# Sliding-window attention and a gated FFN on one core: the second token pair's down projections by the seven-product scheme, with the sums of w_out made in the first pair

## The chip, the core and the metric

The kernel runs on one core of a Trainium2 chip. A core has a matrix engine (TensorE, PE in the profile, with its weight loads as PEld), a vector engine (VectorE, DVE), a scalar engine (ScalarE, ACT), a general engine (GpSimd, POOL) and a sync engine (SyncE, SP) that here issues every DMA. Each engine executes its own queue in order. The metric is the device time of one execution in microseconds; a lower time is better. Three runs of the kernel before took 968.94, 970.25 and 970.04 us, a median of 970.04.

## What is computed

Attention over 8 batches of 8 heads, 576 positions and a head size of 64, where a position sees itself and the 63 before it. Its output, as x with 4608 tokens of 512 features, goes through a gated FFN with 1536 hidden units. Everything is fp32; the weights arrive as 64-bit floats.

```python
scores = scale * np.matmul(q, k.transpose(0, 1, 3, 2))
rel = pos[:, None] - pos[None, :]
scores = np.where((rel >= 0) & (rel < 64), scores, -1e9)
attn = softmax(scores)              # max subtracted, sum + 1e-9
x = (attn @ v).transpose(0, 2, 1, 3).reshape(4608, 512)
gate = 1.0 / (1.0 + np.exp(-(x @ w_gate)))
out = gate * (x @ w_val) @ w_out
```

## The kernel before

**Numbers.** An fp32 product is made of three matmuls on split operands, hi·hi, hi·lo and lo·hi (`three`, the matmul on L612). So each operand is split: ACT casts the high part, DVE subtracts it for the low part (`split`, `x_split`, `h_split`).

**Weights.** w_gate, w_val and w_out come in twelve blocks of 128 rows each. `conv_load`, `conv_a`, `conv_b`, `conv_c` (L102-154) load a block as 64-bit values, turn it into fp32 on ACT and DVE, split it, and store the fp32 form to DRAM (`w32d`) for the sums later. w_out's twelve blocks stay on chip as `wo_all` while tiles 0 and 1 run.

**Tokens.** They go in twelve tiles of 384. A tile's attention is done in units (t, p), tile t and one of four pairs of heads p: scores on PE (`scores`, array s), exponentials (`exponentials`: DVE adds the mask and finds the extreme, L243, ACT takes the exponential, L251), division by the sum (`normalize`: L258, L259, L268), transposes on PE (`stage_b`: L300, out pp) with copies on ACT to pT (L305), and the product with v on PE (`outputs`: L329, out oo), copied to xf (L317). PE keeps its instructions in program order (`pe`).

**First pair.** Tiles 0 and 1 go alone and plainly. `up` (L360, out ph) makes 24 products of a block of hidden units, three rotating PSUM banks serve it; ACT makes the gate (`gate_table`, L369, out g), DVE multiplies and splits (`up_val`, L388; `hidden_split`). `down` (L416, out y) accumulates over the twelve blocks. Tile 0's downs go along with the ups; tile 1's follow at the end, and the hidden activations of its blocks 0 to 9 wait in DRAM for that: `put_hidden` stores the two halves into hd, `get_hidden` loads them as hb. A finished y is copied to yo on ACT (L419) and stored (L420). Units (3,1) and (3,3) of the next pair's attention, and the work that prepares pair 1, are interleaved here.

**Pairs 1 to 5** (two tiles each; `s` in the code). The ups use a scheme of Strassen's kind: a 2x2 block product in seven products (`PRODUCTS`, L429) on sums and differences of blocks. The left operands are blocks and sums S1 to S4 of the weights; the right ones are blocks and sums T1 to T4 of x, made by `x_prep` (DVE: t1 and xf, L566, L567, L574), `x_part` and `x_rest` (splits x_T and x_B, L602, L607). `sums_make` (POOL, out sw), `sums_split` (ACT and DVE or POOL, out ws) and `sums_store` make the weights' sums S from DRAM; they are kept in `wd`. `product` (L639) multiplies and `combine` adds up.

**Downs of the pairs.** Pairs 2 to 5 use the same seven products: the sums of w_out are in DRAM (`wod`), `wo_load` fetches them as wot, `h_prep`, `h_early` and `h_part` make the hidden activations' sums and splits, `last_product` (L751) has 7 x 6 x 2 x 3 = 252 matmuls of 384 columns. Pair 1 does it plainly: `plain_part` splits the activations as h_p, `plain_down` has 24 x 2 x 2 x 3 = 288 such matmuls with `wo_all`, of which blocks 10 and 11 were kept in DRAM (`keep_wo`, `fetch_wo`, array kept and wk). During and after these plain downs `wo_sums_load` and `wo_sums` (L481-490) make the sums of w_out in six blocks k = 0 to 5: two loads of 256 KB (wa), seven DVE and three ACT instructions, eight stores of 128 KB.

**What sets the order.** Every step is entered with a time number (`put`, L781); the list is sorted by these numbers, and the instructions of each engine come out in about that order, with small moves by the scheduler. A tile of a pool (`tag`, `bufs`) is taken again only when the last user of its slot is done. Two tags matter: `w32` (three slots) holds fp32 weights, the yo of tiles 0 and 1, and t1; `raw` (six slots) holds 64-bit weights, hb, sw and the sums of w_out.

## Time and profile before

| what | us |
|---|---|
| median of three runs | 970.04 |
| the profiled execution's own time | 968.12 |
| span of its instructions | 966.3 |
| granted TensorE clock | 1.0 of full speed |
| first pair, until its last down | 0 to 212.5 |
| pair 1's ups | 212.5 to 322.5 |
| pair 1's downs | 322.53 to 372.65 |

The page lists the busy time of each engine with its share of the span and its number of instructions. Groups of instructions (line, engine, operation, output <- inputs, form, count | busy us, mean ns | idle time of the engine just before them and what ended it) tell what a step costs. In a timeline each row is a start, a length, the instruction, and in brackets the idle time before it and what it waited for. Idle time of an engine that does not limit the kernel costs nothing by itself. Of the 19.5 us in which PE is idle, 11.31 lie in the first 40 us (7.54 and 3.77 in its halves), 0.70 between 40 and 80, and 3.55 in the last 47.3 us.

### The profile page before, as it was taken

Reading aid. Unit: us, or ns where it says so; the run is one execution under the profiler, and the core shown is the slowest. Engines: PE = TensorE matmul, PEld = TensorE weight load, DVE = VectorE, ACT = ScalarE, POOL = GpSimd, SP = SyncE. Lnnn points to the kernel's source line nnn. Section 1 sums busy time; section 2 is a strip of 40 time slices with the busy share of each in tenths; the row PEclk is TensorE's granted clock in tenths of the full one; section 3 lists DMA queues with packets and bytes.
Section 4 is the critical chain, followed back from the end, with each engine's and each line's share of the span. In section 5 each row is a group of like instructions: output and inputs, shape, how many; then the busy total and the mean of one; then the engine's idle time right before and its main releaser. Section 6 shows DMA issues by size and latency. Waiting matters only on the chain.

```text
span 966.3 us, 20552 instructions
## 1 busy us (share of the span) xinstructions
PE 946.8 (98%) x7200; PEld 904.1 (94%) x7200; DVE 692.8 (72%) x1873; ACT 597.3 (62%) x1479; POOL 141.8 (15%) x232
## 2 busy tenths in 40 slices
PE   6899999999999999999999999999999999999998
PEld 4798999889999999999999999999999999999998
DVE  7889989756776964666876666796566697567782
ACT  7888877647787644666754666664666675222350
POOL 4200103327661000110100111100110100000000
PEclk9999999999999999999999999999999999999999
DMA  9899999948998868889989888878888868988464
GB/s 344 313 384 356 398 353 346 395 165 290 319 305 283 287 205 265 279 259 323 342 265 301 285 257 271 262 258 284 293 264 259 262 212 263 306 252 257 142 211 160
DMA packets 110838, 272.41 MB, mean 282 GB/s; under 512 B 12048, under 2 KB 42896, under 8 KB 110736
## 3 DMA queue, kind: packets, MB, share of 16 engines
q1 hardware_dynamic: 110736, 271.11, 83.2%
q8 instruction: 57, 0.93, 0.4%
q14 instruction: 45, 0.37, 0.1%
HBM read 214.17 MB, written 56.89 MB: 280 GB/s over the span
## 4 chain that ended last, share of the span: by engine, by line
PE 82%; ACT 6%; DVE 5%; DMA 3%; issue 2%; POOL 1%; SPq 0%; DVEq 0%; ACTq 0%
PE pr L612 39%; PE y L612 23%; PE ph L360 6%; PE y L416 4%; PE s L219 3%; PE pp L300 2%; PE s L329 2%; ACT p L251 2%; DMA a<-w32d 1%; DMA w32d<-w 1%; PE oo L329 1%; ACT L251 1%; ACT pT L305 1%; PE pr L329 1%; ACT L369 1%
## 5 line engine op out<-in xcount | busy, mean ns | idle before, releaser
L612 PE MATMUL pr<-x_T,wt 128*128 128x384 f32 x1224 | 227.9, 338 | 0.0
L612 PEld LDWEIGHTS pr<-x_T,wt 128*128 128x128 f32 x1224 | 211.3, 188 | 4.2 <-issue 2.6
L612 PE MATMUL pr<-x_B,wt 128*128 128x384 f32 x1008 | 187.5, 336 | 0.0
L612 PE MATMUL y<-h,wot 128*128 128x384 f32 x1008 | 176.0, 334 | 0.0
L612 PEld LDWEIGHTS pr<-x_B,wt 128*128 128x128 f32 x1008 | 175.0, 188 | 0.6 <-DMA wt<-wd 0.3
L612 PEld LDWEIGHTS y<-h,wot 128*128 128x128 f32 x1008 | 174.6, 188 | 0.5 <-DVE h L655 0.3
L268 POOL TENSOR_TENSOR p<-p,rs 128x384 f32<-128x384 f32 x76 | 66.4, 888 | 567.5 <-DVE rs L259 511.2
L720 ACT CAST h<-h 128x384 fp32r<-128x384 f32 x168 | 82.6, 515 | 67.2 <-PE y L612 34.4
L251 ACT ACTIVATE p<-p,mn 128x128 f32<-128x128 f32 x288 | 111.0, 394 | 6.2 <-DVE mn L243 5.6
L360 PE MATMUL ph<-x,w 128*128 128x384 f32 x576 | 106.2, 338 | 0.1
L721 DVE TENSOR_TENSOR h<-h,h 128x384 fp32r<-128x384 f32 x168 | 88.6, 553 | 24.1 <-ACT h L720 22.7
L360 PEld LDWEIGHTS ph<-x,w 128*128 128x128 f32 x576 | 99.7, 188 | 2.4 <-issue 0.9
L243 DVE CUSTOM_DVE_ANT_0 p<-s,m 128x128 f32<-128x128 f32 x288 | 65.7, 286 | 38.8 <-PE s L219 38.5
L369 ACT ACTIVATE g<-c 128x384 f32<-128x384 f32 x90 | 46.6, 524 | 69.1 <-DVE c L651 68.8
L655 DVE TENSOR_TENSOR h<-c,g 128x384 f32<-128x384 f32 x90 | 55.9, 621 | 29.8 <-ACT g L369 25.5
L369 ACT ACT_TABLE_LOAD x40 | 51.3, 1283 | 13.4 <-DVE c L651 12.8
L305 ACT COPY pT<-pp 128x384 f32<-128x384 f32 x96 | 41.4, 480 | 28.2 <-PE pp L300 28.1
L219 PE MATMUL s<-k,q 64*64 64x128 f32 x1152 | 46.0, 287 | 7.7 <-DMA k<-in_kT_dram 4.9
L622 DVE TENSOR_TENSOR c<-pr,p 128x384 f32<-128x384 f32 x60 | 33.1, 551 | 27.7 <-PE pr L612 27.7
L251 ACT ACT_TABLE_LOAD x39 | 50.0, 1283 | 0.7
L251 ACT ACTIVATION_READ_ACCUMULATOR p<-p,mn 128x1 f32 x264 | 49.9, 189 | 0.0
L219 PEld LDWEIGHTS s<-k,q 64*64 64x64 f32 x1152 | 33.4, 138 | 14.3 <-DMA q<-in_qT_dram 5.2
(113 smaller groups left out, 1326.8 us busy)
## 6 DMA issues: line engine op xcount, KB each, us to landing
wt<-wd SPq DMA_DIRECT2D x186, 512.0 KB, 4.5
wot<-wod SPq DMA_DIRECT2D x84, 512.0 KB, 4.4
v<-in_vN_dram SPq DMA_DIRECT2D x48, 384.0 KB, 5.2
wd<-ws SPq DMA_DIRECT2D x48, 256.0 KB, 4.7
k<-in_kT_dram SPq DMA_DIRECT2D x48, 224.0 KB, 5.2
q<-in_qT_dram SPq DMA_DIRECT2D x48, 192.0 KB, 5.0
w32d<-w SPq DMA_DIRECT2D x36, 256.0 KB, 5.2
wd<-w SPq DMA_DIRECT2D x36, 256.0 KB, 5.6
```

The source lines that it names most:

```text
L219: pe(nc.tensor.matmul(sc[h][half * BLK:(half + 1) * BLK, u, :], qt[h * BLK:(h + 1) * BLK, U * BLK:(U + 1) * BLK], kt[h * BLK:(h + 1) * BLK ...
L243: nc.vector.tensor_tensor_reduce(out=pt[:, u, :], in0=sc[:, u, :], in1=masks[key], op0=ALU.add, op1=ALU.min, scale=-SCALE, scalar=3.0e38, ...
L251: exp = nc.scalar.activation(pt[:, u, :], pt[:, u, :], AF.Exp, bias=mn[:, u:u + 1], scale=-1.0, **sums)
L268: eng.tensor_mul(out=pt, in0=pt, in1=rs.unsqueeze(2).broadcast_to([P, UP, P]))
L305: cp = nc.scalar.copy(pT, pp)
L329: pe(nc.tensor.matmul(oo[U // 2][h * BLK:(h + 1) * BLK, U % 2 * BLK:(U % 2 + 1) * BLK], vt[:, U, h * BLK:(h + 1) * BLK], pT[h][:, U // 2, ...
L360: pe(nc.tensor.matmul(ph, l, r, start=i == 0, stop=i == len(prs) - 1))
L369: act = nc.scalar.activation(g, c, AF.Sigmoid)
L612: pe(nc.tensor.matmul(ps, l, r, start=first and i == 0, stop=last and i == 2, skip_group_check=not check))
L655: nc.vector.tensor_mul(out=hidden(s, k)[2 * r + b], in0=c, in1=gates.pop((t, j)))
L720: nc.scalar.copy(h2[:, 0, :], src)
L721: nc.vector.tensor_sub(out=h2[:, 1, :], in0=src, in1=h2[:, 0, :].bitcast(F32))
```

## The change

Pair 1's downs go by the seven products too, so `plain_part`, `plain_down`, `keep_wo` and `fetch_wo` go. For this the sums of w_out have to be ready earlier: blocks 0 to 3 are put at the end of the first pair, blocks 4 and 5 into pair 1's ups. The plain parts of w_out (`wo_parts`) are stored right after the conversion of their block. The hidden activations of tile 1's blocks 0 to 9 stay on chip: `hidden_split` writes them into slots x10 to x13, e0 to e4 and one of raw, and `put_hidden` and `get_hidden` go. Pair 1 gets the calls of `h_prep`, `h_early`, `h_part` and `wo_load` that the other pairs have.

```diff
+            wo_parts(j)
...
-    hd = dr.tile([NF, P, 2, TT], F32, name="hd")
+    KEEP = 2
...
+        if t == 1 and j < NF - KEEP:
+            pool, tag, bufs = (xp, f"x{10 + j}", 1) if j < 4 else (xp, f"e{j - 4}", 1) if j < 9 else (mp, "raw", RAW)
+            h2 = pool.tile([P, 2, TT], F32R, name=f"h2_{t}_{j}", tag=tag, bufs=bufs)
+            h_hi, h_lo = h2[:, 0, :], h2[:, 1, :]
...
-
-    def put_hidden(t, j):
-        h_hi, h_lo = hh.pop((t, j))
-        nc.sync.dma_start(out=hd[j, :, 0, :], in_=h_hi.bitcast(F32))
-        nc.sync.dma_start(out=hd[j, :, 1, :], in_=h_lo.bitcast(F32))
-
-    def get_hidden(t, j):
-        if j > 5:
-            hb = xp.tile([P, 2, TT], F32R, name=f"hb_{t}_{j}", tag=f"x{10 + (j + 2) % 4}")
-        else:
-            hb = mp.tile([P, 2, TT], F32R, name=f"hb_{t}_{j}", tag="raw", bufs=RAW)
-        nc.sync.dma_start(out=hb.bitcast(F32), in_=hd[j])
-        hh[(t, j)] = (hb[:, 0, :], hb[:, 1, :])
...
-        with tc.issue_after(marks["w_load"]) if s == 2 else nullcontext():
+        with tc.issue_after(marks["w_load"]) if s == 1 else nullcontext():
             nc.sync.dma_start(out=w2.bitcast(F32), in_=wod[q])
...
+    def wo_parts(j):
+        for name, half in (("A12", 0), ("A22", 1)) if j % 2 else (("A11", 0),):
+            nc.sync.dma_start(out=wo_at(j // 2, name),
+                              in_=wo_all[j][:, :, half * H:(half + 1) * H].bitcast(F32))
+
+    def wo_sums_tile(k, n, i):
+        if k < 4:
+            return mp.tile([P, n, DM], F32, name=f"wq{i}_{k}", tag="raw", bufs=RAW)
+        if i is None:
+            return mp.tile([P, n, DM], F32, name=f"wq{i}_{k}", tag="w32", bufs=W32)
+        return wts.tile([P, n, DM], F32, name=f"wq{i}_{k}", tag=f"wo_{i}")
...
-        a = mp.tile([P, 2, DM], F32, name=f"wa_{k}", tag="raw", bufs=RAW)
+        a = wo_sums_tile(k, 2, 5)
         for i in range(2):
-            nc.sync.dma_start(out=a[:, i, :], in_=w32d[2][k + i * NK])
+            with tc.issue_after(marks["conv_load"]):
+                nc.sync.dma_start(out=a[:, i, :], in_=w32d[2][k + i * NK])
...
-        b = mp.tile([P, 4, H], F32, name=f"wb_{k}", tag="raw", bufs=RAW)
-        c = mp.tile([P, 2, H], F32, name=f"wc_{k}", tag="raw", bufs=RAW)
+        b = wo_sums_tile(k, 2, 6).rearrange("p i (a h) -> p (i a) h", a=2)
+        c = wo_sums_tile(k, 1, None).rearrange("p i (a h) -> p (i a) h", a=2)
...
-    def keep_wo(pos):
-        nc.sync.dma_start(out=kept[pos], in_=wo_all[pos].bitcast(F32))
-
-    def fetch_wo(pos):
-        w2 = wts.tile([P, 2, DM], F32R, name=f"wk_{pos}", tag="W", bufs=WB)
-        nc.sync.dma_start(out=w2.bitcast(F32), in_=kept[pos])
-        wo_all[pos] = w2
...
-    def plain_part(i):
-        b, x = divmod(i, NF)
-        k, r = PLAIN[x]
-        hs[i] = h_split(f"p{i}", i, hidden(1, k)[2 * r + b])
...
-    def plain_down(i, part):
-        b, x = divmod(i, NF)
-        k, r = PLAIN[x]
-        for d in ((2, 3) if (part == 1) != (x == NF - 1) else (0, 1)):
-            at, q = (2 * b, 1)[d // 2], d % 2
-            if x == 0:
-                acc[q][at] = psum(1 + q, at, f"y{b}_{d}")
-            ps = acc[q][at][:, :TT]
-            three(ps, wo_all[2 * k + r], d, hs[i], x == 0, x == NF - 1)
-            if x == NF - 1:
-                yo = mp.tile([P, TT], F32, name=f"yo_{b}_{d}", tag="g", bufs=4)
-                nc.scalar.copy(yo, ps)
-                nc.sync.dma_start(out=outT[d * P:(d + 1) * P, b * TT:(b + 1) * TT], in_=yo)
...
-            if t == 1 and j < NF - KEEP:
-                put(now, 9.1, put_hidden, t, j)
...
-        for n, j in enumerate(js):
-            put(now + n * DNT - ready[0], 9.4, ready[1], t, j)
...
-    for x, pos in enumerate(KEPT):
-        put(now - 14 + 4 * x, 8.6, keep_wo, pos)
+    for k in range(NK):
+        put(now - 32 + 10 * k if k < 4 else now + 80 + 8 * (k - 4), 7, wo_sums_load, k)
+        put(now - 24 + 10 * k if k < 4 else now + 88 + 8 * (k - 4), 7, wo_sums, k)
...
-                put(now + 12, 8.6, wo_parts, k)
...
-            if s > 1:
-                put(now + 0.5, 5, h_prep, s, k)
-                if k < EXTRA:
-                    put(now + 3, 5.1, h_early, s, k)
+            put(now + 0.5, 5, h_prep, s, k)
+            if k < EXTRA:
+                put(now + 3, 5.1, h_early, s, k)
...
-        if s == 1:
-            for pos in KEPT:
-                put(t0 - 4, 7, fetch_wo, pos)
-            for i in range(2 * NF):
-                for part in range(2):
-                    at_down.append(now)
-                    put(now, 9, plain_down, i, part)
-                    now += PRT
-                    attend(("d", 2 * i + part))
-            for i in range(2 * NF):
-                put(at_down[2 * i - 38] + 2.3 if i > 18 else t0 - 14.5 if i < EXTRA else t0 - 14.5 + 2.1 * ((i - 5) // 2 + 1) if i < 8
-                    else t0 - 4 if i == 8 else t0 - 0.5, 5.2, plain_part, i)
-            x_parts(at_down[14], lambda x: at_down[max(10 + 2 * x, 18 + x)] + 2.4)
-            for k in range(NK):
-                put(at_down[24] + 4 + 11 * k, 7, wo_sums_load, k)
-                put(at_down[24] + 12 + 11 * k, 7, wo_sums, k)
-            continue
...
-                put(at_down[i - 13] + 1.1 if i > 13 else t0 - 80 + 4 * i if s > 2 else t0 - 48 + 3 * i, 8.2, wo_load, s, i // 2)
+                put(at_down[i - 13] + 1.1 if i > 13 else t0 - 80 + 4 * i if s > 1 else t0 - 18 + 2 * i, 8.2, wo_load, s, i // 2)
```

How it moves instructions, at three places (line numbers behind an L are each kernel's own; a name ends in a running number).

PE at the start of pair 1's downs. In the names y0_0 are a product's sums, h_p0 a plain split of activations, w2_2 a block of w_out on chip. Before:

```order
L612 MATMUL y0_0_4746<-h_p0_4541,w2_2_1172 128x384 x3
L612 MATMUL y0_1_4750<-h_p0_4541,w2_2_1172 128x384 x3
L612 MATMUL y0_2_4754<-h_p0_4541,w2_2_1172 128x384 x3
L612 MATMUL y0_3_4758<-h_p0_4541,w2_2_1172 128x384 x3
L612 MATMUL y0_0_4746<-h_p1_4544,w2_3_1322 128x384 x3
L612 MATMUL y0_1_4750<-h_p1_4544,w2_3_1322 128x384 x3
```

After (h_0_1_0: the first product's activations of pair 1, block 0; wot_1_0: w_out's parts loaded for pair 1):

```order
L599 MATMUL y0_0_1_4839<-h_0_1_0_3469,wot_1_0_4567 128x384 x3
L599 MATMUL y0_1_1_4843<-h_0_1_0_3469,wot_1_0_4567 128x384 x3
L599 MATMUL y0_0_1_4839<-h_0_1_1_3779,wot_1_0_4567 128x384 x3
L599 MATMUL y0_1_1_4843<-h_0_1_1_3779,wot_1_0_4567 128x384 x3
L599 MATMUL y0_0_1_4839<-h_0_1_2_4056,wot_1_1_4649 128x384 x3
L599 MATMUL y0_1_1_4843<-h_0_1_2_4056,wot_1_1_4649 128x384 x3
```

A block of activations has two output tiles instead of four, and the weights come from loads. PE's order is unchanged everywhere else.

ACT between the exponentials of unit (3,1) and its copies to pT. ws0_1_0 and ws2_1_0 are the sums of w_val's block 0, p0_3_1 and p1_3_1 the two halves of the unit's softmax, g the gates. Before:

```order
L251 ACT_TABLE_LOAD
L251 ACTIVATE p0_3_1_2561,rs_3_1_2563<-p0_3_1_2561,mn0_3_1_2562 128x128 x3
L251 ACTIVATE p1_3_1_2573,rs_3_1_2563<-p1_3_1_2573,mn1_3_1_2574 128x128
L157 CAST w2_10_2502<-w32_2_10_2449 128x512
L251 ACTIVATE p1_3_1_2573,rs_3_1_2563<-p1_3_1_2573,mn1_3_1_2574 128x128 x2
L369 ACT_TABLE_LOAD
L369 ACTIVATE g_0_11_2620<-ph0_0_11_2607 128x384
L117 ACTIVATE w32_2_11_2622<-raw_2_11_2545 128x512
L546 CAST ws0_1_0_2929<-sw_1_0_2803 128x2x256
L546 CAST ws2_1_0_2932<-sw_1_0_2803 128x2x256
L157 CAST w2_10_2502<-w32_2_11_2622 128x512
L369 ACTIVATE g_1_11_2688<-ph0_1_11_2675 128x384
```

After (wq6, wq5 and wqNone are the three tiles of a block of w_out's sums, here block 1):

```order
L533 CAST ws2_1_0_2923<-sw_1_0_2783 128x2x256
L370 ACT_TABLE_LOAD
L370 ACTIVATE g_0_11_2603<-ph0_0_11_2590 128x384
L370 ACTIVATE g_1_11_2673<-ph0_1_11_2660 128x384
L589 CAST x_B11_1_0_2881<-xf_2_0_1308 128x384
L589 CAST x_B21_1_0_2939<-xf_2_2_1536 128x384
L589 CAST x_B11_1_1_3008<-xf_2_1_2245 128x384
L589 CAST x_B21_1_1_3069<-xf_2_3_2511 128x384
L482 CAST wq6_1_2945<-wq6_1_2945 128x512
L485 CAST wqNone_1_2946<-wq5_1_2845 128x256
L486 CAST wqNone_1_2946<-wq5_1_2845 128x256
L306 COPY pT0_3_1_2702<-pp0_3_1_2698 128x384
```

The two casts of ws stood behind the exponentials and the gate of block 11; now the first stands ahead of the table load for the exponentials and the second ahead of that for the gate. The three casts of block 1's sums stand ahead of the copies to pT, which nothing of the kind did before.

DVE at the division of unit (3,3), whose quotient PE transposes next. rs is the sum of the exponentials, p0 and p1 the two halves, t1 and xf the differences for pair 1's x, x_T their splits. Before:

```order
L258 SCALAR_TENSOR_TENSOR rs_3_3_2782<-rs_3_3_2782 128x3
L259 RECIPROCAL rs_3_3_2782<-rs_3_3_2782 128x3
L268 TENSOR_TENSOR p0_3_3_2780<-p0_3_3_2780,rs_3_3_2782 128x384
L258 SCALAR_TENSOR_TENSOR rs_3_3_2782<-rs_3_3_2782 128x3
L259 RECIPROCAL rs_3_3_2782<-rs_3_3_2782 128x3
L268 TENSOR_TENSOR p1_3_3_2792<-p1_3_3_2792,rs_3_3_2782 128x384
L566 TENSOR_TENSOR t1_1_0_2868<-xf_3_0_1760,xf_2_0_1316 128x384
L567 TENSOR_TENSOR xf_3_0_1760<-xf_3_2_2029,xf_3_0_1760 128x384
L574 TENSOR_TENSOR xf_2_0_1316<-xf_3_2_2029,t1_1_0_2868 128x384
L607 TENSOR_TENSOR x_T1_1_0_2908<-t1_1_0_2868,x_T1_1_0_2908 128x384
L566 TENSOR_TENSOR t1_1_1_2986<-xf_3_1_2764,xf_2_1_2262 128x384
```

After (p1_3_3's multiplication stands two rows behind the last one shown):

```order
L553 TENSOR_TENSOR t1_1_0_2863<-xf_3_0_1748,xf_2_0_1308 128x384
L269 TENSOR_TENSOR p0_3_3_2760<-p0_3_3_2760,rs_3_3_2762 128x384
L259 SCALAR_TENSOR_TENSOR rs_3_3_2762<-rs_3_3_2762 128x3
L554 TENSOR_TENSOR xf_3_0_1748<-xf_3_2_2017,xf_3_0_1748 128x384
L561 TENSOR_TENSOR xf_2_0_1308<-xf_3_2_2017,t1_1_0_2863 128x384
L553 TENSOR_TENSOR t1_1_1_2999<-xf_3_1_2744,xf_2_1_2245 128x384
L488 TENSOR_TENSOR wq5_2_2983<-wq5_2_2983,wqNone_2_3076 128x256
L489 TENSOR_TENSOR wq5_2_2983<-wq5_2_2983,wqNone_2_3076 128x256
L260 RECIPROCAL rs_3_3_2762<-rs_3_3_2762 128x3
L594 TENSOR_TENSOR x_T1_1_0_2899<-t1_1_0_2863,x_T1_1_0_2899 128x384
L594 TENSOR_TENSOR x_T3_1_0_2930<-xf_3_0_1748,x_T3_1_0_2930 128x384
L594 TENSOR_TENSOR x_T2_1_0_2891<-xf_2_0_1308,x_T2_1_0_2891 128x384
```

t1_1_0 and the work behind it stood after both multiplications; now t1_1_0 stands ahead of p0's and, with the second t1, two rows of block 2's sums and four x_T, ahead of p1's. t1_1_0 takes the slot of the tile yo_0_0 (tag w32), t1_1_1 that of yo_0_1. The store of yo_0_0 stands in SP's queue, before:

```order
L403 DMA hb_1_5_2825<-hd_149 128x768
L455 DMA wd_0_3_153<-ws2_1_0_2932 128x512
L455 DMA wd_0_6_156<-ws2_1_0_2932 128x512
L442 DMA wt_1_0_4_2977<-wd_0_4_154 128x1024
L500 DMA kept_11_214<-w2_10_2502 128x1024
L465 DMA wod_14_206<-w2_10_2502 128x2x256
L465 DMA wod_17_209<-w2_10_2502 128x2x256
L442 DMA wt_1_0_5_3002<-wd_0_5_155 128x1024
L420 DMA out_0_dram<-yo_0_0_2734 128x512
L190 DMA v_4_0_2959<-in_vN_dram 128x768
```

and after:

```order
L470 DMA wq5_2_2983<-w32d_2_2_139 128x512
L470 DMA wq5_2_2983<-w32d_2_8_145 128x512
L434 DMA wt_1_0_5_3014<-wd_0_5_154 128x1024
L492 DMA wod_6_197<-wq6_1_2945 128x256
L492 DMA wod_3_194<-wq6_1_2945 128x256
L492 DMA wod_9_200<-wqNone_1_2946 128x256
L492 DMA wod_18_209<-wqNone_1_2946 128x256
L412 DMA out_0_dram<-yo_0_0_2713 128x512
L412 DMA out_0_dram<-yo_0_1_2722 128x512
```

Ahead of it four stores of block 1's sums and two loads for block 2 have come in, and the loads of hb and the copy to kept have gone.

## Prediction

> **What bounds the kernel now.** I read the busy times first.

> ```profile
> span 966.3 us, 20552 instructions
> PE 946.8 (98%) x7200; PEld 904.1 (94%) x7200; DVE 692.8 (72%) x1873; ACT 597.3 (62%) x1479; POOL 141.8 (15%) x232
> ```

> PE works 946.8 of 966.3 us, so only 19.5 us are idle. Next the windows show where (after the window: its length, then busy time of PE, PEld, DVE, ACT, POOL, granted clock, DMA share, GB/s).

> ```profile
> 160.00:180.00 20.00, 20.00 (x150) 18.39 (x149) 19.25 (x46) 14.36 (x33) 11.12 (x19) 1.00 1.03 378
> 180.00:200.00 20.00, 19.78 (x152) 15.83 (x151) 10.48 (x34) 11.19 (x31) 0.70 (x2) 1.00 0.99 375
> 200.00:213.00 13.00, 13.00 (x79) 10.53 (x78) 8.04 (x24) 5.72 (x20) 4.47 (x7) 1.00 0.17 54
> 300.00:322.50 22.50, 22.50 (x190) 21.53 (x189) 19.35 (x52) 18.52 (x46) 0.00 (x0) 1.00 0.81 282
> 322.50:373.00 50.50, 50.50 (x293) 50.50 (x292) 32.59 (x76) 21.71 (x49) 0.00 (x0) 1.00 0.66 210
> 482.00:526.00 44.00, 44.00 (x254) 44.00 (x255) 33.03 (x67) 22.64 (x47) 0.00 (x0) 1.00 0.86 278
> ```

> From 160 us to the end of pair 1's downs PE is nearly never idle. A matmul taken out there is worth its whole time; a wait put in there costs its whole length. At the end of the first pair (160 to 180) PE is full, DVE has 0.75 us free and the DMA engines are full too. That is where the change puts its new work.

> **What the change takes out.** Third, the chain of waits (start, length, what): pair 1's downs, then pair 2's, which already go by seven products.

> ```profile
> 322.53 50.12 PE y L612 x288
> 481.95 43.88 PE y L612 x252
> ```

> 288 matmuls become 252: 36 × 50.12/288 = 6.27 us by the pair's own price, 50.12 − 43.88 = 6.24 us by pair 2's. I take **−6.24 us**. Pair 2's phase runs with no gap, from parts and weights that are made in the same places of its own ups, and the changed pair 1 has the same order of parts. The recombination (DVE adds, ACT copies) and the further splits lie under PE, as in pair 2's phase, whose window (482 to 526) has PE busy throughout with DVE at 33.03 of 44.00 us. The w_out sums leave pair 1's phase, which is worth nothing, since PE did not wait for them (50.50 of 50.50).

> **What it adds, and where.** Each of the six blocks of w_out sums has these DVE and ACT instructions (six blocks: x6; busy us, mean ns).

> ```profile
> L488 DVE TENSOR_TENSOR wb<-wb 128x512 f32<-128x512 f32 x6 | 4.1, 688 | 0.2
> L481 DVE TENSOR_TENSOR wb<-wa 128x256 f32<-128x256 f32 x6 | 2.5, 424 | 14.4 <-DMA wa<-w32d 14.4
> L483 ACT CAST wb<-wb 128x512 fp32r<-128x512 f32 x6 | 3.7, 622 | 17.3 <-DVE wb L482 14.7 <-issue 2.6
> L487 ACT CAST wc<-wa 128x256 fp32r<-128x256 f32 x6 | 2.4, 403 | 0.2 <-DVE wa L485 0.2
> ```

> One block is six of 0.42 and one of 0.69 us on DVE, 3.2 us, and 0.62 + 2 × 0.40 = 1.4 us on ACT, with ten DMA issues. Blocks 3 to 5 run behind the last softmax step of the first pair or in pair 1's ups, after a stretch (200 to 213) with a DMA share of 0.17 and DVE busy 8.04 of 13 us; I count nothing for them, and should that cover be gone a block costs its 3.2 us. Blocks 0 to 2 stand in the DVE queue among the last softmax steps of the first pair, and PE's next steps hang on those. Two places matter.

> First, unit (3,1): PE's last two steps for it, and ACT's copies between.

> ```profile
> 179.88 0.82 PE L300 MATMUL pp<-ident,p 128*128 128x128 f32 x6
> 182.80 0.92 PE L329 MATMUL oo<-pT,v 128*64 128x64 f32 x24
> 181.62 0.86 ACT L305 COPY pT<-pp 128x384 f32<-128x384 f32 x2
> 182.36 1.09 ACT L419 COPY yo<-y 128x512 f32<-128x512 f32 x2
> 176.35 0.62 ACT L546 CAST ws<-sw 128x512 fp32r<-128x512 f32 x1 [1.17 <-POOL sw L534]
> ```

> In the new ACT order the first cast of ws_1_0, which waited for POOL here (1.17 us), stands ahead of the exponentials of (3,1), and block 1's three casts (1.4 us) ahead of the pT copies. I put the pT copies 1.9 us later, at 183.5: PE loses 1 to 1.5 us at its oo step, and the copy of the first output yo_0_0 ends near 184.8.

> Second, unit (3,3), the larger term. PE wants its normalised p at 193.42; DVE had finished it 4.5 us before, and then waited for a store of yo_0_0, because the tile t1 takes the store's buffer.

> ```profile
> 193.42 0.82 PE L300 MATMUL pp<-ident,p 128*128 128x128 f32 x6
> 188.42 0.56 DVE L268 TENSOR_TENSOR p<-p,rs 128x384 f32<-128x384 f32 x1
> 195.20 0.56 DVE L566 TENSOR_TENSOR t<-xf,xf 128x384 f32<-128x384 f32 x1 [6.23 <-DMA out_dram<-yo]
> 195.80 0.56 DVE L567 TENSOR_TENSOR xf<-xf,xf 128x384 f32<-128x384 f32 x1
> 196.27 0.55 DVE L574 TENSOR_TENSOR xf<-xf,t 128x384 f32<-128x384 f32 x1
> 188.13 0.63 SPq L420 DMA_DIRECT2D out_dram<-yo  x1
> ```

> The store went out at 188.13 and let t1 go at 195.20, 7.07 us later. In the new order of DVE t1 stands **in front of** both multiplications of p_3_3, so a wait that cost nothing is now ahead of PE's need. Between t1's start and the end of p1_3_3's multiplication stand t1, p0's multiplication, two xf, the second t1 and four x_T (nine of 0.53 by the steps from 195.20 to 196.27, 4.8 us), two block-2 sums (0.8), two short ones (0.4) and p1's own 0.56: 6.6 us. PE reaches p1's transposes at 193.42 + 0.41 = 193.83. If t1 starts at T, PE stands for T + 6.6 − 193.83 = **T − 187.2 us**.

> T is when yo_0_0's store is done, and SP's one queue decides that.

> ```profile
> 170.56 1.26 SPq L455 DMA_DIRECT2D wd<-ws  x2
> 168.11 4.04 POOL L553 TENSOR_TENSOR ws<-sw,ws 128x128 fp32r<-128x128 f32 x8 [6.42 <-ACT ws L546]
> ```

> From the first store of ws_0_0 (170.56) to yo_0_0's (188.13) SP issued 21 DMAs, 6.75 MB by their sizes, in 17.57 us. After the change 32 stand there, smaller, 7.0 MB: the hb loads and the copies to "kept" go, 12 stores of sums and four loads for them come. By the bytes the stretch keeps its length, but it starts earlier: POOL idled 6.42 us before it splits ws_0_0, for a cast that now stands earlier on ACT; I give it 4 us of that. Then the store could go at 184.1, and the copy (184.8) bounds it: issue at about 185.5, T = 185.5 + 7.07 = 192.6, and the stall is 5.4 us. The 1 to 1.5 us at (3,1) are inside it, since T does not move with PE.

> The bounds: with the landing of the quickest load below (4.4 us) T is 189.9 and the stall 2.7 us; with the copy as early as now (182.36 + 0.56) and a landing of 5.2 us T is 188.1 and the stall 0.9 us. From above, T as before, 195.20, gives 8.0 us, and rival D more. I take 5.4: its landing is that of the very same store. (Columns below: KB each, median us to landing.)

> ```profile
> wot<-wod SPq DMA_DIRECT2D x84, 512.0 KB, 4.4
> w32d<-w SPq DMA_DIRECT2D x36, 256.0 KB, 5.2
> hb<-hd SPq DMA_DIRECT2D x10, 384.0 KB, 5.7
> L416 PE MATMUL y<-w,hb 128*128 128x512 f32 x90 | 21.3, 393 | 0.0
> ```

> The round trip of the activations through DRAM (hd, loaded as hb) costs PE nothing today: the matmuls that read hb have 0.0 us of idle time ahead of them. Keeping h on chip therefore gains only room in SP's queue, which is counted above.

> One more price: two-input DVE instructions while POOL works.

> ```profile
> 199.30 1.39 POOL L532 TENSOR_TENSOR sw<-a 128x128 f32<-128x128 f32 x2 [21.69 <-DVE t L566]
> 201.76 0.81 DVE L607 TENSOR_TENSOR x_T<-t,x_T 128x384 fp32r<-128x384 f32 x1
> 198.13 0.56 DVE L607 TENSOR_TENSOR x_T<-t,x_T 128x384 fp32r<-128x384 f32 x1 [1.30 <-ACT x_T L602]
> ```

> Beside POOL's sums the same x_T takes 0.81 instead of 0.56 us. If POOL's sw_0_1 falls onto the eight rows ahead of p1, that is 8 × 0.25 = 2.0 us more; its loads now stand behind block 2's stores on SP, later than those rows, so I leave it out of the sum and in the range. [...]

> **The sum.** −6.24 + 5.4 = −0.8 us: 967.3 for an execution like the profiled one (968.12, its span 966.3), which lies 1.92 under the median of 970.04; on the median, **969.2 us**. A measurement of this kernel can tell about 0.2% (1.94 us) from no change, so this is "within".

> **Rivals.**

> A, the forecast: T between 191.5 and 195.4, stall 4.3 to 8.2, time 968.1 to 972.0. For it: t1's place in DVE's order and the 6.23 us wait are both there. Chance 0.45.

> B, the store lands early or p1 is not delayed: stall under 4.3. With T = 189.9 the time is 970.04 − 6.24 + 2.7 = 966.5; with no stall at all 963.8. For it: SP loses 384 and 512 KB transfers, and stores of the old sums landed in 2.0 us once the queue was light. Against: the DMA share is 0.99 from 180 to 200. Chance 0.30.

> ```profile
> wod<-wb SPq DMA_DIRECT2D x24, 128.0 KB, 2.0
> ```

> [...]

> C, the change does not do what it says: pair 1's downs do not reach 43.88 us, because the weights of sums 4 and 5, made late in its ups, come late. DVE is busy 19.35 of 22.5 us there, the fullest stretch of the pair. Each such wait gives back 1 to 3 us on top of A. It is inside the chances of A and D.

> D, slower, one mechanism: the 32 rows in SP's queue go at the old pace for each DMA, 17.57/21 = 0.84 us, not at the old pace for bytes. From 166.6 the store then goes at 193.4, T = 200.5, the stall is 13.3 us and the time 970.04 − 6.24 + 13.3 = 977.1. It decides from T = 195.4 on (stall 8.2 us, the store issued after 188.3); half way, T = 197, gives 973.6. For it: waits for a full queue stretch SP's issues here (1.26 us for two). Against: the new stores have half the size. Chance 0.25.

> **How the numbers follow.** Likeliest is A, at 969.2. B below 965.0 holds about 0.08 and D above 973.5 about 0.12, so the range is 965.0 to 973.5; it takes in stalls from 1.2 to 9.7 us. Faster by over 0.2% (under 968.1) is B, 0.30; within, A, 0.45; slower (over 972.0), D, 0.25.

> **What will show it.** Pair 1's downs: one piece of 252 matmuls of about 43.9 us in the chain; over 45 is C. PE's row of transposes after 36 y matmuls, near 195 to 200: an idle time of 4 to 6 us that ends with the DVE multiplication of p, and DVE's t row just before it with a wait for the output's store. If that t row shows no wait, or PE no gap there, A is wrong and B holds. If the store's issue on SP comes after 188.3, D holds. A gap of more than 2 us at oo of (3,1) would make the first place the larger one.

## The result, and the profile after

The changed kernel takes **982.45 us** (median of four runs, 980.19 to 984.12) beside 969.49 us before on the same chip: ratio 1.0132 with a 95% interval of 1.0109 to 1.0155. It is slower, and lies above the forecast range of 965.0 to 973.5 us. The profiled execution took 982.93 us, its span is 981.1. The head of the page:

```profile
span 981.1 us, 20488 instructions
PE 951.8 (97%) x7164; PEld 906.6 (92%) x7164; DVE 720.7 (73%) x1925; ACT 604.1 (62%) x1493; POOL 146.3 (15%) x232
```

PE's busy time should have fallen by the 6.24 us of the removed matmuls, to 940.6 us. It rose to 951.8, so the 36 matmuls are gone and the others took 11.2 us more; and PE is idle 29.3 us instead of 19.5. The chain of waits (start, length, what) says that the removal itself went as forecast:

```profile
343.13 43.88 PE y L599 x252
```

Pair 1's downs are one piece of 252 matmuls of 43.88 us, but it starts at 343.13 instead of 322.53: 20.6 us were lost ahead of it. The windows show three of the places (window: length, busy time of PE, PEld, DVE, ACT, POOL, granted clock, DMA share, GB/s):

```profile
60.00:80.00 20.00, 16.48 (x122) 14.65 (x121) 17.84 (x43) 15.97 (x37) 2.07 (x2) 0.91 1.03 362
160.00:180.00 20.00, 16.89 (x116) 15.21 (x115) 17.60 (x31) 10.26 (x20) 13.47 (x22) 0.83 0.82 282
300.00:322.50 22.50, 20.77 (x150) 19.77 (x149) 17.50 (x51) 17.16 (x49) 7.93 (x16) 0.92 0.84 283
```

From 160 to 180 us PE was busy 20.00 of 20 us before; now it is 16.89, and the granted clock, 1.00 in every window of before that was shown, is 0.83. What PE waits for, first in before and then in the changed kernel, from 60 to 340 us (us in all, times, longest):

```profile
PE s L219 <- ACT xf L317: 1.6, 3, 1.0
PE s L329 <- ACT pT L305: 0.6, 1, 0.6
PE pr L612 <- DVE ws L548: 0.6, 1, 0.6
```

```profile
PE s L220 <- ACT xf L318: 4.4, 3, 3.4
PE oo L330 <- ACT pT L306: 3.1, 2, 2.7
PE pr L599 <- DVE ws L535: 2.1, 2, 1.7
PE s L330 <- ACT pT L306: 2.0, 2, 1.7
PE pp L301 <- DVE p L269: 1.4, 1, 1.4
```

The place of the forecast, pp waiting for DVE's p, is the smallest of the five. To date the loss, I compare the starts of PE's transposes (pp) of the same unit in both traces:

| stretch | before, us | after, us | lost |
|---|---|---|---|
| 67.4 to 160.4 in before: place A | 93.07 | 98.91 | +5.8 |
| 160.4 to 179.9: place B | 19.44 | 25.69 | +6.25 |
| 179.9 to 216.7: with unit (3,3), the place of the forecast | 36.86 | 38.31 | +1.45 |
| 216.7 to 316.7: pair 1's ups | 99.95 | 106.94 | +7.0 |
| 316.7 to 381.9: with pair 1's downs | 65.17 | 58.95 | −6.2 |

**Place A.** ACT's timeline of the changed kernel, then the row of before that answers to its last one (start, length, instruction, in brackets the idle time before it):

```profile
74.97 0.66 ACT L117 ACTIVATE w<-raw 128x512 f32<-128x512 f32 x1
75.83 0.62 ACT L158 CAST w<-w 128x512 fp32r<-128x512 f32 x1 [0.20 <-DVE w L130]
76.35 0.68 ACT L118 ACTIVATE raw<-raw 128x512 int32<-128x512 uint32 x1
76.92 0.46 ACT L318 COPY xf<-oo 128x384 f32<-128x384 f32 x1
```

```profile
73.41 0.46 ACT L317 COPY xf<-oo 128x384 f32<-128x384 f32 x1
```

Steps of weight conversion, one of which waits for DVE, now stand between the end of PE's input (73.71) and the copy of unit (2,0), for which PE waits: the copy starts 3.2 us after that end, where before it started 0.2 us after it. PE's rows here and at place B:

```profile
77.43 1.55 PE L220 MATMUL s<-k,q 64*64 64x128 f32 x22 [3.36 <-ACT xf L318]
171.92 0.47 PE L330 MATMUL oo<-pT,v 128*64 128x64 f32 x2 [2.69 <-ACT pT L306]
```

**Place B** is the second row. ACT at that place:

```profile
167.30 0.62 ACT L158 CAST w<-w 128x512 fp32r<-128x512 f32 x1 [2.36 <-DVE w L130]
169.75 0.67 ACT L117 ACTIVATE w<-raw 128x512 f32<-128x512 f32 x1 [1.83 <-DMA raw<-in_moe_w_out_dram]
171.39 0.48 ACT L306 COPY pT<-pp 128x384 f32<-128x384 f32 x1
```

(Two more steps, from 170.33 to 171.49, stand between the last two rows.) The conversion of w_out's block 11 waits there for its load, and the copy of pT for unit (2,3), which needs nothing of it, stands behind. In before it ran as soon as PE had made its input, ahead of that conversion:

```profile
160.97 0.86 ACT L305 COPY pT<-pp 128x384 f32<-128x384 f32 x2 [1.24 <-PE pp L300]
```

**The clock.** Each of the four longest waits from 60 to 340 us (3.36, 2.69, 1.66 and 1.73 us) is followed by matmuls at half clock. The rows of single microseconds (length, PE busy, granted clock, DMA share, GB/s):

```profile
75.00:76.00 1.00, 0.00 (x0) 1.00 0.93 340
76.00:77.00 1.00, 0.00 (x0) 0.68 0.93 369
82.00:83.00 1.00, 1.00 (x4) 0.50 1.00 386
83.00:84.00 1.00, 1.00 (x7) 0.91 1.02 379
171.00:172.00 1.00, 0.08 (x1) 0.96 0.91 319
267.00:268.00 1.00, 1.00 (x26) 0.75 0.50 139
308.00:309.00 1.00, 0.86 (x3) 0.73 0.82 281
```

0.68 in a microsecond means half clock from 76.36 on, 0.91 means until 83.18: 6.82 us. In the same way the others begin at 171.92 (6.83 us), 267.50 (3.41) and 308.46 (3.41). Together 20.5 us at half clock, of which PE stood still for 1.5: some 9.5 us lost, most of the 11.2. With the 9.8 us of more idle time and the gain of 6.24 this makes the difference of the spans.

### The profile page after: what moved, and what is told of

Read it like the earlier page. It is cut to its first block, busy times and chain, and to the rows that moved or that the text cites. A ratio compares the mean times of both kernels' runs of the same rounds, so it can differ in the third digit from the quotient of the medians.

```text
span 981.1 us, 20488 instructions
## 1 busy us (share of the span) xinstructions
PE 951.8 (97%) x7164; PEld 906.6 (92%) x7164; DVE 720.7 (73%) x1925; ACT 604.1 (62%) x1493; POOL 146.3 (15%) x232
## 4 chain that ended last, share of the span: by engine, by line
PE 68%; ACT 12%; DVE 10%; DMA 4%; issue 3%; SPq 0%; DVEq 0%; ACTq 0%
PE pr L599 33%; PE y L599 22%; ACT p L252 4%; PE s L220 3%; PE ph L361 3%; PE y L408 2%; ACT L370 2%; PE s L330 2%; PE pp L301 2%; ACT L252 2%; DMA w32d<-w 1%; ACT g L370 1%; DVE w L130 1%; DVE c L638 1%; DVE h L642 1%
## 5 line engine op out<-in xcount | busy, mean ns | idle before, releaser
L599 PE MATMUL y<-h,wot 128*128 128x384 f32 x1260 | 219.9, 334 | 0.0
L599 PEld LDWEIGHTS y<-h,wot 128*128 128x128 f32 x1260 | 218.2, 188 | 0.6 <-DVE h L642 0.3
L681 ACT CAST h<-h 128x384 fp32r<-128x384 f32 x210 | 103.1, 514 | 83.6 <-PE y L599 42.3
L682 DVE TENSOR_TENSOR h<-h,h 128x384 fp32r<-128x384 f32 x210 | 111.0, 555 | 28.8 <-ACT h L681 28.0
L220 PE MATMUL s<-k,q 64*64 64x128 f32 x1152 | 47.7, 294 | 11.5 <-DMA k<-in_kT_dram 6.0
L220 PEld LDWEIGHTS s<-k,q 64*64 64x64 f32 x1152 | 34.8, 142 | 18.5 <-DMA q<-in_qT_dram 5.3
## 6 DMA issues: line engine op xcount, KB each, us to landing
wt<-wd SPq DMA_DIRECT2D x186, 512.0 KB, 4.5
wot<-wod SPq DMA_DIRECT2D x105, 512.0 KB, 4.8
v<-in_vN_dram SPq DMA_DIRECT2D x48, 384.0 KB, 5.1
wd<-ws SPq DMA_DIRECT2D x48, 256.0 KB, 4.7
w32d<-w SPq DMA_DIRECT2D x36, 256.0 KB, 4.8
wd<-w SPq DMA_DIRECT2D x36, 256.0 KB, 6.2
```

The source lines that it names most:

```text
L220: pe(nc.tensor.matmul(sc[h][half * BLK:(half + 1) * BLK, u, :], qt[h * BLK:(h + 1) * BLK, U * BLK:(U + 1) * BLK], kt[h * BLK:(h + 1) * BLK ...
L599: pe(nc.tensor.matmul(ps, l, r, start=first and i == 0, stop=last and i == 2, skip_group_check=not check))
L681: nc.scalar.copy(h2[:, 0, :], src)
L682: nc.vector.tensor_sub(out=h2[:, 1, :], in0=src, in1=h2[:, 0, :].bitcast(F32))
```

## The experiments

All times but that of the six gaps are medians beside runs of before on the same chip, and losses are by the stretches of the table above. Each edit is shown by a few of its lines alone. I held theory **O**: without the stores of the activations ACT's order changes, and A and B follow from that order alone. The rival **S**: the sums of w_out, made early, take the place on DVE, ACT and SP.

**Only the activations kept on chip** (before, without its stores and loads of hd, nothing of the sums):

```
-    put(now, 9.1, put_hidden, t, j)
+    h2 = pool.tile([P, 2, TT], F32R, name=f"h2_{t}_{j}", tag=tag, bufs=bufs)
```

> The kernel before with one part of the change alone: the hidden activations of tile 1's blocks 0 to 9 stay on chip, and their stores and loads go; the sums of w_out and pair 1's plain downs stay as before. Theory O (order: with the twenty stores gone, the scheduler puts the weight conversions of the first pair ahead of the pT and xf copies in ACT's queue, and PE waits there): the two gaps of the change's profile come back, PE 5 to 6 us later from 75 to 91 us and another 6 us from 166 to 192, and with no gain in the downs the time is 969.5 + 11.4 = about 981 us. Rival S (the early sums of w_out load DVE, ACT and SP at the end of the first pair): no sums stand there, so no gap, 968 to 970.5 us.

979.94 us, 1.0097 (1.0071 to 1.0123). A loses 5.4 us, B 4.4, the rest 1.5. The part of the change that I had priced at nothing makes 9.8 of the 12.1 us at A and B by itself, which is about half of what the changed kernel loses ahead of the downs.

**The round trip put back, the sums as changed:**

```
+    put(now + n * DNT - ready[0], 9.4, ready[1], t, j)
```

> The changed kernel with the round trip of the hidden activations through DRAM put back; the early sums and pair 1's seven-product downs stay. Theory O: no gap at 75 to 91 nor at 166 to 192; what stays is the loss of some 1.5 us at unit (3,3) and of some 7 us in pair 1's ups, so 969.5 - 6.2 + 1.5 + 7 = about 972 us, and below 966 if the loss in the ups also goes. Rival S: the gap at 166 to 192 stays, with the loss in the ups 969.5 - 6.2 + 6.2 + 8.5 = about 978 us.

981.14 us, 1.0109 (1.0086 to 1.0132). Both theories missed the total, but A and B are gone (−0.4 and 0.0 us), as O said. Instead (3,3) loses 3.5 and pair 1's ups 15.3 us, with three stretches of half clock in them (3.41 us each, from 235.20, 245.44 and 306.88 us): there is a second cause, in the ups.

**The changed kernel with the 20 stores again, which nobody reads:**

```
+    def put_hidden(t, j):
+        nc.sync.dma_start(out=hd[j, :, 0, :], in_=h_hi.bitcast(F32))
+        nc.sync.dma_start(out=hd[j, :, 1, :], in_=h_lo.bitcast(F32))
```

> The changed kernel, hidden activations on chip as in the change, with the twenty stores to DRAM issued as well though nobody reads them. It does more work than the change. Theory O: the stores alone bring ACT's order of the first pair's middle back, so no gap at 75 to 91, and the time falls by 5 us or more against the change, to 970 to 977 us. Rival B (the buffers that the activations hold on chip are what delays the weight loads): the gaps stay and the time is that of the change, 982 us, or a little above.

972.83 us, 1.0031 (1.0020 to 1.0042): 9.6 us less than the changed kernel, with 20 DMAs more. A loses 0.0, B 1.5 and (3,3) 1.3; the ups still lose 7.1, with a granted clock of 1.00 throughout.

**The sums made in pair 1's ups:**

```
-    put(now - 32 + 10 * k if k < 4 else now + 80 + 8 * (k - 4), 7, wo_sums_load, k)
+    put(now + 20 + 14 * k, 7, wo_sums_load, k)
```

> The changed kernel with all six blocks of sums of w_out in pair 1's ups (one block each 14 us of the order's numbers), none in the first pair. Theory O: the gap at 75 to 91 stays at 5 to 6 us and that at 166 to 192 for the most part, as ACT's order there keeps the conversions ahead of the copies; the ups lose as much as before or more, 978 to 986 us. Rival S: the gap at 166 to 192 and the wait at unit (3,3) go, so 982.5 - 7.7 = about 975 us.

1005.66 us, 1.0365 (1.0340 to 1.0391), a miss. A and B stay, so the sums don't cause them; but the weights come too late for the downs, whose wait says it:

```profile
PE y L597 <- DMA wot<-wod: 18.7, 1, 18.7
```

**A and B by order alone, first try** (the weight conversion held behind ACT's copy, at two places):

```
+    HOLD = {6: ("xf", 2, 2), 11: ("pT", 2, 3)}
+    behind.enter_context(tc.issue_after(marks[("copy",) + HOLD[j]]))
```

> The changed kernel, no stores added, with one constraint on ACT: the conversion of w_gate's and w_val's block 6 may not stand ahead of the copy xf of unit (2,2), and w_out's block 11 not ahead of the pT copies of unit (2,3). If ACT's order alone makes the gaps, the one at 75 to 91 us goes (-5.3) and that at 166 to 192 shrinks or goes (0 to -4, since three other casts still stand ahead there): 973 to 977 us. If it is not the order but the queue of transfers that the missing stores change, it stays at 982 us.

978.79 us, 1.0090 (1.0075 to 1.0105), a miss: B fell from 6.25 to 1.2 us, but I had held the wrong unit at A, which is (2,0) and not (2,2), and A rose from 5.8 to 7.7.

**The same with the right unit:**

```
+    HOLD = {(3, 2, "a"): ("xf", 2, 0), (4, 1, "c"): ("xf", 2, 0),
+            (4, 2, "a"): ("xf", 2, 0), (11, 2, "a"): ("pT", 2, 3)}
```

> The changed kernel with one difference of order: the ACT conversions of w_out's blocks 3 and 4 and the cast of the value weights' block 4 stand behind the copy of xf_2_0, and the activations of w_out's block 11 stand behind the copies of pT of unit (2,3); nothing is added or left out. Theory O (ACT's order costs 5.7 us at 67 to 91 us and 6.25 us at 160 to 192 us): both go but for about 1 us at the second, 982.4 - 5.7 - 5.2 = 971.5 us (970 to 973.5), and the gap at L220 of the first falls from 3.36 us to under 1 us. Rival (the conversions' place is only where another shortage shows, and the gap moves): 975 us or more.

973.37 us, 1.0032 (1.0017 to 1.0047): 9.1 us less than the changed kernel, with the same instructions. A is 1.2, B 0.7 us. ACT and PE at A:

```profile
74.24 0.47 ACT L319 COPY xf<-oo 128x384 f32<-128x384 f32 x1
```

```profile
74.76 0.88 PE L220 MATMUL s<-k,q 64*64 64x128 f32 x22 [1.12 <-ACT xf L319]
```

The copy starts 1.0 us after PE has made its input (73.28) instead of 3.2, the wait falls from 3.36 to 1.12 us (0.35 in before), and the 22 matmuls take 0.88 instead of 1.55. That ACT's order causes A and B is shown. That it hangs on the stores is shown as well; why the scheduler, which goes by its own times, orders ACT so without them, I did not look into.

**The ups, without the sums** (dead stores; every load of w_out's sums reads a part that is there, so that the sums of w_out are left out):

```
-    put(now - 24 + 10 * k if k < 4 else now + 88 + 8 * (k - 4), 7, wo_sums, k)
```

> The kernel of the dead stores without any sums of w_out: their loads, DVE and ACT instructions and stores are left out, and the downs load written parts in their place (the output is not the reference's; the downs of all pairs use wrong weights of the same size). If the sums' own work costs what the dead stores' kernel still loses (2.8 us at the end of the first pair, 7 us in pair 1's ups), those losses go and the time is the forecast gain alone, 969.9 - 6.2 = 963.7, at most 965.5 us. If the preparation of the hidden activations that pair 1's ups now hold costs the 7 us, they stay, and the time is 968 to 971 us.

969.95 us, 1.0002 (0.9993 to 1.0011). The ups still lose 6.8 us: the sums are not what fills them. One row of DVE, and some of POOL's beside it, stand out:

```profile
224.46 4.82 DVE L648 TENSOR_TENSOR h<-c,g 128x384 f32<-128x384 f32 x1
```

```profile
223.82 1.72 POOL L546 TENSOR_TENSOR ws<-sw,ws 128x128 fp32r<-128x128 f32 x4
225.49 0.87 POOL L525 TENSOR_TENSOR sw<-a 128x128 f32<-128x128 f32 x2
227.98 0.89 POOL L531 TENSOR_TENSOR sw<-a,sw 128x128 f32<-128x128 f32 x2
```

This multiplication takes 0.56 us elsewhere. POOL worked without a pause from 218.8 to 228.9, and it ended 0.4 us later. Such a row need not be dear: in the run with the activations alone one took 5.03 us, and its ups lost 1.6.

**Block 5's sums sooner** (dead stores; on DVE block 5 moves from 291 to 305 us to 238 to 262, blocks 4 and 5 still stand in the ups):

```
+    put(now - 32 + 10 * k, 7, wo_sums_load, k)
```

> The kernel of the dead stores with blocks 4 and 5 of the sums 10 us of the order's numbers apart from the others (as blocks 0 to 3 are) instead of late in pair 1's ups. In DVE's queue only block 5 moves, from the fifth to the second of the six steps of the ups. If the sums' place in DVE's and SP's queues makes the loss in the ups, the wait near 298 us (2.3 us, the sums of w_val late) goes and the time falls by 2 to 5 us against the dead stores' 972.8, to 968 to 971; if it is their mere work, the time stays within 1.5 us of 972.8.

974.27 us, 1.0043 (1.0027 to 1.0060): the ups lose 10.3 us, more than the 7.1 with block 5 late. So the late place of block 5 does not make the loss; a kernel with dead stores and all six blocks ahead of the ups was not run.

**Without the sums and without the subtractions of the hidden activations** (both are left out, the products read the plain activations):

```
-        differences(nc.vector, b11, b12, b22, t1)
```

> The kernel with the dead stores and without the sums of w_out, and with pair 1's three subtractions for each k (differences, T2) left out as well: 18 of DVE's two-input operations less while pair 1's ups run; the products read the plain activations in their place. Theory H (these subtractions hold up DVE's serving of the ups): of the 6.8 us lost there in the kernel without sums at least 4 go, 963.5 to 966 us. Rival (the splits into high and low halves, which stay, or the earlier order of ACT hold it up): 968 to 970.5 us, the stretch from 230 to 337 us still over 4 us longer than before's.

969.41 us, 0.9991 (0.9979 to 1.0004): hardly a gain over the run without sums (969.95), so it isn't these instructions alone. The ups lose 5.1 us in this trace, and again one row of DVE lasts until POOL, busy from 238.9, stops at 249.0; this one has six elements for each partition:

```profile
245.90 3.10 DVE L259 SCALAR_TENSOR_TENSOR rs<-rs 128x6 f32<-128x6 f32 x1 [1.65 <-ACT p L252]
```

**Without POOL's sums, in the kernel with the two holds** (POOL's work on the gate and value weights of pair 1 is left out, the casts read the loaded weights):

```
-            nc.gpsimd.tensor_add(out=sw[:, 0, c], in0=a2[:, c], in1=a2[:, d])
+        sw = [a.rearrange("p (a h) -> p a h", a=2) for a in (a1, a2)]
```

> The kernel with the two holds on ACT (973.4 us), with all of POOL's work on the gate and value weights' sums in pair 1 left out: the casts read the loaded weights in place of the sums, and the gate's low halves are read from the high ones. DVE's and ACT's instructions stay. Theory C (in pair 1's ups the added work loses time because POOL's sums hold up DVE's two-input instructions, and because the casts of ws wait for POOL): of the 7.9 us that the stretch from unit (3,3) to the downs is longer than before's at least 5 go, 966 to 968.5 us, and no two-input DVE instruction is over 1 us there. Rival (DVE and ACT have too much to do in the ups by themselves): over 4 us of the 7.9 stay, 970.5 us or more.

976.10 us, 1.0063 (1.0040 to 1.0086), a miss in the total. In the middle of the ups, from the transposes at 216.74 to those at 303.47 in before, it lost 1.2 us where the kernel with the holds lost 5.4. That is what theory C expects of this part, but I chose the part afterwards; by the numbers that I had named the rival came true, for from (3,3) to the downs the kernel lost 12.0 us, where C had under 3. Two other waits came up:

```profile
199.48 0.52 PE L301 MATMUL pp<-ident,p 128*128 128x128 f32 x3 [2.60 <-DVE p L269]
325.86 3.67 PE L592 MATMUL pr<-x_T,ws 128*128 128x384 f32 x12 [3.92 <-DVE u L602]
```

At the first, (3,3), block 2's sums and t1 stand ahead of p on DVE; at the second, block 5's sum, which waits 2.34 us for its load, and the subtractions of h stand ahead of u. With the half clock behind both (3.41 us each, from 200.23 and 326.52) they took back more than was won.

**Without the sums and without POOL's** (the kernel with the dead stores; both left out):

```
-        put(now - 24 + 10 * k if k < 4 else now + 88 + 8 * (k - 4), 7, wo_sums, k)
-            nc.gpsimd.tensor_add(out=sw[:, 0, c], in0=a2[:, c], in1=a2[:, d])
```

> The kernel with the dead stores and without the sums of w_out (969.95 us; between unit (3,3) and the downs it takes 6.8 us more than before), with POOL's work on pair 1's weight sums left out too: the casts read the loaded weights in place of the sums. What pair 1's ups then have that before's don't is the subtractions and splits of the hidden activations on DVE and ACT. Theory C (POOL's sums hold up DVE, and ws waits for them): under 2.5 us of the 6.8 stay, no two-input DVE instruction over 1.5 us there, 964.5 to 966.5 us. Rival (DVE and ACT are too full by themselves): over 4 us stay, 968 us or more.

963.76 us, 0.9943 (0.9926 to 0.9961): 6.2 us less than with POOL's sums, and about the gain of the downs below before. The ups lose 1.6 us, and B, where the run without the sums still lost 1.7, loses nothing. The ups as one window, first in before, then in the changed kernel, then without the sums, then without POOL's as well:

```profile
216.70:316.70 100.00, 98.57 (x837) 93.58 (x836) 70.30 (x206) 75.56 (x195) 52.85 (x112) 1.00 0.89 301
```

```profile
230.30:337.30 107.00, 102.23 (x837) 96.31 (x835) 86.22 (x236) 77.44 (x203) 57.27 (x112) 0.97 0.90 308
```

```profile
218.20:324.90 106.70, 100.98 (x835) 94.94 (x834) 82.78 (x220) 74.84 (x195) 56.55 (x112) 0.98 0.83 280
```

```profile
216.60:318.20 101.60, 99.36 (x837) 93.38 (x836) 73.25 (x220) 74.72 (x195) 0.00 (x0) 1.00 0.87 293
```

The matmuls are the same (835 to 837 records). The same 220 DVE instructions take 82.78 us beside POOL and 73.25 without it, 9.5 us more, and PE's stretch is 5.2 us longer. The casts of ws no longer wait for POOL in that kernel; how much of the 5.2 us is that and how much the slower DVE, no run tells apart. Before has as much of POOL's work in its ups (52.85 us) but not the added work on DVE: POOL's sums and the added work cost little each without the other, and 6.8 us together.

**The clock by itself** (before, with ACT copies in place between two halves of a product, 1, 2, 3, 4, 6 and 9 of them, at six places):

```
+    STALL = {(2, 1, 3): 1, (2, 5, 3): 2, (3, 1, 3): 3, (3, 5, 3): 4, (4, 1, 3): 6, (4, 5, 3): 9}
+    nc.scalar.copy(part, part.bitcast(F32))
```

> The kernel before, with 1, 2, 3, 4, 6 and 9 ACT copies of a 128x128 piece in place between the two halves of one product, at six places of the later pairs' downs some 20 us or more apart, so that PE stands still for some 0.8 to 2.6 us there. Theory G (a gap of about 1.5 us or more is followed by some microseconds at half clock): the places with 4 copies or more show granted clock 0.5 in the microseconds behind the gap and cost 2 to 3 us more than the gap, those with 1 to 3 copies cost their gap alone; the whole is 14 to 18 us longer than before. Rival (the half clock of the earlier runs came from what PE did there, not from the gap): no clock below 1.0 in these stretches, some 8 to 10 us longer.

981.37 us in a single run beside 969.20. The waits were 0.39, 0.77, 1.05, 1.43, 2.04 and 3.08 us, and theory G failed in this form: only the last was followed by half clock. PE's rows of the two longest, and the clock behind the last:

```profile
805.69 25.24 PE L612 MATMUL y<-h,wot 128*128 128x384 f32 x144 [2.04 <-ACT h L762]
834.01 2.49 PE L612 MATMUL y<-h,wot 128*128 128x384 f32 x9 [3.08 <-ACT h L762]
```

```profile
834.00:835.00 1.00, 0.99 (x5) 0.98 0.01 4
835.00:836.00 1.00, 1.00 (x5) 0.50 0.14 37
```

144 matmuls behind the wait of 2.04 us took 25.24 us, 0.175 each, as the 252 of 43.88 us do at a granted clock of 1.00, though waits of 1.66 and 1.73 us in the changed kernel had been followed by half clock. What decides is told in the last section.

## Why the prediction was wrong

**The gain was right.** "I take −6.24 us" for 288 matmuls that become 252: 43.88 us measured, and within 0.4 us of it in every run of these downs that had its weights in time.

**The step that failed most** is "The round trip of the activations through DRAM … costs PE nothing today … Keeping h on chip therefore gains only room in SP's queue". That it gains nothing by itself was right. But I priced what goes as if all else stayed where it was. Without the 20 stores the order of ACT came out another way at two places, where weight conversions moved ahead of copies that PE waits for: 5.8 and 6.25 us. I had read the changed order of DVE and ACT only where the sums of w_out stand; A lies 100 us before them. The run with the activations alone, the one with dead stores and the one with two holds show it from three sides.

**The price of a wait.** "A matmul taken out there is worth its whole time; a wait put in there costs its whole length" was too low for long waits. A's wait of 3.36 us and B's of 2.69 and 0.42 cost 5.8 and 6.25, because 6.8 us at half clock went with each (some 2.9 and 3.2 us, half of the time that PE worked in them).

**The term at (3,3) was mis-sized.** Forecast: 5.4 us. DVE, SP and PE at that place in the changed kernel:

```profile
201.61 0.53 DVE L553 TENSOR_TENSOR t<-xf,xf 128x384 f32<-128x384 f32 x1
202.06 0.55 DVE L269 TENSOR_TENSOR p<-p,rs 128x384 f32<-128x384 f32 x1
206.62 0.55 DVE L269 TENSOR_TENSOR p<-p,rs 128x384 f32<-128x384 f32 x1
```

```profile
195.44 2.40 SPq L412 DMA_DIRECT2D out_dram<-yo  x3
```

```profile
207.31 0.52 PE L301 MATMUL pp<-ident,p 128*128 128x128 f32 x3 [1.36 <-DVE p L269]
```

The order is as forecast, t1 ahead of both multiplications, and 5.6 us lie between the start of the first t1 and the end of p1's multiplication, where I had 6.6. But t1's row shows no wait: the store landed at 200.26, 4.8 us after its issue instead of 7.07. PE came 12.0 us late by A and B; less that, t1 started at 189.6, where I had 192.6. Those 3.0 us and the 1.0 us of shorter work are why 1.36 us of waiting were left of 5.4: by the sign that I had named, rival B held here. At (3,1), where I had 1 to 1.5 us, PE's oo step shows no wait. Across the runs in which A and B are mostly gone the stretch with (3,3) lost −0.1 us without the sums of w_out and 1.3 to 4.8 us with them, the most where p1 waited 2.60 us.

**The ups, which I had counted as nothing**, lost 7.0 us. "Blocks 3 to 5 run … in pair 1's ups … I count nothing" rested on DVE's free time there, and "the changed pair 1 has the same order of parts" on pair 2's ups. There POOL has next to nothing to do, as their window in before shows (13.51 of 108.90 us; 52.85 of 100.00 in pair 1's):

```profile
373.00:481.90 108.90, 108.43 (x935) 103.48 (x934) 74.54 (x228) 73.84 (x201) 13.51 (x16) 1.00 0.91 311
```

In the changed kernel PE waits 4.7 us in the ups instead of 1.2, 2.1 of them for ws and 2.0 for pT, and two steps of half clock take 3.4 more: that is the 7.0. DVE's work there rose from 70.30 to 86.22 us, and by the times of the runs without POOL (0.42, 0.69 and 0.55 us each) the 30 instructions more make some 15 of these 15.9. So the price that I had left out of the sum, DVE's two-input instructions beside POOL (0.81 instead of 0.56 us at one row), adds little to this rise. Shown is that without POOL's sums the loss falls from 6.8 to 1.6 us in the kernel without the sums of w_out. For the kernel with the two holds the run without POOL shows it for the middle of the ups alone (5.4 to 1.2 us); what its last 13 us and (3,3) would cost with another order of DVE was not tried.

One path that the experiments leave open is SP's order. Four more stores of ws and one more load stand ahead of the last load for POOL's sums, which in before goes out ahead of them. First the load in before, then in the changed kernel, and POOL behind it:

```profile
276.87 0.32 SPq L522 DMA_DIRECT2D a<-w32d  x1
```

```profile
298.17 0.38 SPq L509 DMA_DIRECT2D a<-w32d  x1
302.41 0.88 POOL L519 TENSOR_TENSOR sw<-a 128x128 f32<-128x128 f32 x2 [3.81 <-DMA a<-w32d]
```

Counted from the start of each one's stretch, the load goes out 7.7 us later and POOL begins its last block 6.2 us later (at 282.57 in before); PE's wait of 1.73 us for ws, with a step of half clock behind it, follows at 308.14. No run has this order alone put back, so how much of the 7.0 us hangs on it stays open.

**Rivals.** C did not hold for the downs (43.88). D's sign came true, the store's issue at 195.44 being after 188.3, but less the 12.0 us of A and B it is 183.4. SP took 22.5 us for the 32 rows, between the 17.6 of the forecast and D's 26.8, and PE waited 1.36 us where D has 13.3. That the time came out on D's side, slower, is therefore luck. None of the rivals had the order of ACT in it.

No kernel tried beats before while it computes everything; the nearest is the changed one with dead stores, 972.83 us. The 963.76 us are a bound on what there is to win if pair 1's weight sums stayed off POOL while the ups run: that run leaves out the sums of w_out too, and whatever the sums would cost elsewhere.

## What to carry to other kernels

When a change takes instructions away from a program that a scheduler orders, compare the order of every engine from the first instruction that is gone, not only where new ones stand: what PE waits for can move behind work that it doesn't need. Price a wait of PE at up to its length and, where half clock follows it, 1.7 us more for each step of 3.41 us that PE works at half clock: in the changed kernel that was so behind the waits of 1.66 to 3.36 us, in other runs not behind those of 2.04 and 2.27 us. Work that costs nothing by an engine's free time can still be dear where it meets another engine's work on the same chain: here the added work on DVE lost 1.6 us without POOL's sums and 6.8 us beside them.

## What the runs showed of the hardware

**Single DVE instructions lasted up to 5 us beside POOL.** 4.82 us for a multiplication of 0.56, and 3.10 for a step on 128x6, both ended within 0.5 us of a pause of POOL. The traces have three more such rows in pair 1's ups (5.03 us with the activations alone, 1.78 with the six gaps, 1.46 in before), all at the end of some 10 us of unbroken work on POOL. In the two runs without POOL's sums no DVE row there takes over 0.7 us. It is not the rule: in the changed kernel, with POOL at work, the longest DVE row of the ups takes 0.95 us. The size of one such block is what I had not expected: the forecast's price beside POOL was 0.25 us a row (0.81 instead of 0.56).
